# Fused attention, dense layer and eight experts: float32r and bf16 words become pairs of float16 parts

## The chip, the core and the metric

The kernel runs on one core of a Trainium2 chip (trn2). A core has TensorE (PE, with its weight loads shown apart as PEld), VectorE (DVE), ScalarE (ACT), GpSimd (POOL) and SyncE (SP, which here mostly starts transfers), and 16 DMA engines. The metric is the time of one execution on the device in microseconds.

## The reference

Three parts follow each other; the output of one is the input of the next, always with 1152 tokens of 512 numbers.

```python
# attention: batch 2, 8 heads, 576 positions, head size 64
scores = scale * np.matmul(q, k.transpose(0, 1, 3, 2))
cum = np.cumsum(np.maximum(s, 0.0), axis=-1)
bias = -(cum[:, :, :, None] - cum[:, :, None, :])
scores = np.where(causal, -1000000000.0, scores + np.minimum(bias, 0.0))
x = softmax(scores) @ v
# dense layer, 512 -> 2048 -> 512; w_in and w_out arrive as 64-bit floats
h = x @ w_in
x2 = (h * (1.0 / (1.0 + np.exp(-1.702 * h)))) @ w_out
# experts: the best of 8 for each token, at most 288 tokens each
expert_idx = np.argmax(x2 @ w_gate, axis=1)
y = np.maximum(disp @ w1, 0.0) @ w2          # 512 -> 1024 -> 512
out[i] = gate_w[i] * y[expert_idx[i], pos[i]]
```

The results have to be close to float32, so that the kernel splits numbers into parts, and a product of two numbers is made of three products of parts: high by high, high by low, and low by high.

## The kernel before

**How the order is made.** The program text calls `pl.op(engine, cost, function, r=, w=, rank=)`. Class `Plan` collects these operations, takes the dependences from the keys in `r` and `w`, and a list scheduler with modelled costs writes each engine's instructions in the order that it finds: among the operations that are ready, the one with the lowest rank goes first. Ranks come from the stage (`n + 0.5`, `base + 15` and the like) plus a table `SHIFT` of hand-tuned offsets. On the chip each engine then goes through its own list in that order, and waits for others by semaphores.

**Attention** (0 to about 130 us) works on 8 pairs of heads. A `unit` takes one pair and one tile of queries t (64 rows for t=0, 128 for t=1 to 4): PE makes the scores in float32 (`score_mm`, L863, and the causal mask with L864), DVE takes the maximum (L885), ACT the exponential (`pexp`, L894), and the result is split into two float16 parts in the tile `ph` (L846 and L848, with POOL or DVE at L908 and L913). SP sends `ph` through a DMA transpose into `PT` (L921), in blocks of 128x128, and `av_unit` multiplies by the values (L941, float16). Two heads give 128 columns; PE transposes them (L965), and three copies go to `xT` (high and low, float32r) and `xTb` (bf16, L846).

**Dense layer** (92 to about 330 us). The 1152 tokens are three chunks of 384, the 2048 inner numbers 16 blocks of 128. `mm1` for a chunk c and a block fc runs 8 float32r matmuls of 384 columns (L577, high weights by high and low x) and 4 bf16 matmuls (L581, low weights by high x), then ACT tanh, DVE, ACT high part, DVE low part (L585 to L591), and one more ACT copy in bf16 (`gtB`, L594). `mm2` runs for each tile of 128 tokens two float32r matmuls of 512 columns (L610) and one of bf16 (L611). There are 48 of the former and 144 of the latter. `w_conv` makes each block of weights out of 64-bit words with bit operations on ACT and DVE and a subtraction on POOL or DVE (L536 to L553). `logits` transposes a tile of x2, copies it to SBUF and multiplies by `w_gate` in float32 (L1208). `route` counts and sends rows to the memory `xs_d`.

**Experts** (335 to 470 us) come sorted by their number of tokens, with compiled widths WR = (224, 200, 184, 168, 152, 144, 136, 128). `w_unit` loads 512 KB pieces of weights in a ring of buffers, ACT makes the high part (L1455) and DVE the low part (L1456). `xs_in` fetches an expert's rows (x2R<-xs_d), transposes and splits them (L1535 on). `e_mm1` has 8 units an expert, `e_mm2` 4. Their float32r matmuls hold high and low side by side, 2w columns (L1569, L1606), the bf16 matmuls the narrower width that the run has counted, by a register on PE (`widths`, `held`, L1573, L1608). Afterwards the halves of PSUM are added: ACT copies one half (L1583), DVE adds (L1585), ACT relu (L1587), DVE low part (L1589), ACT bf16 copy (L1592). `e_mm2` is left by ACT (L1613) and DVE (L1615). The last expert is computed by rows (`e_row`, L1634), ending in `e_out_row` (L1669) and an indirect DMA (L1642). Behind all of it stands a branch for experts with more tokens than the compiled width (L1738), which isn't taken.

## Time and profile before

| | us |
|---|---|
| median of three executions | 487.0 |
| the three | 487.0, 2492.14, 484.84 |
| profiled execution | 485.11 |
| its span | 483.4 |
| PE busy | 458.7 |
| DVE, ACT, POOL busy | 362.7, 332.4, 122.9 |

The span lasts from the first to the last instruction recorded on the core; the profiled execution's own time has the start and end around it too. PE means matmuls; a weight load can run beside the matmul before it, so the two don't add up. "PEclk" is the clock granted to TensorE as a share of 2.4 GHz. "DMA" is the share of the time in which the 16 DMA engines were busy. The chain of waits is made backwards from the last instruction: each piece is the work that the next one waited for.

### The profile page before, as it was taken

The page shows a single profiled execution, that of the slowest core. Times are in us where ns is not written, and L with a number is a line of the kernel's source. Part 1 is how long each engine was busy: PE and PEld are TensorE (multiplying, and loading weights), DVE is VectorE, ACT ScalarE, POOL GpSimd, SP SyncE. Part 2 cuts the span into 40 slices and gives each one's busy share as a digit, 9 for nine tenths or more (in the row PEclk, how much of TensorE's full clock was granted, in tenths as well). Part 3 has the DMA queues.
Part 4 walks back from the last instruction along what each step waited for, and adds up shares of the span by engine and source line. Part 5 has one row for each costly group of instructions (what it writes and reads, how often), then busy time and mean ns, then how long its engine had stood idle before and what let it go on. Part 6 is the DMA issues. An engine that isn't in the chain of part 4 may idle for free.

```text
span 483.4 us, 9843 instructions
## 1 busy us (share of the span) xinstructions
PE 458.7 (95%) x3458; PEld 349.3 (72%) x3460; DVE 362.7 (75%) x826; ACT 332.4 (69%) x785; POOL 122.9 (25%) x136
## 2 busy tenths in 40 slices
PE   8898898999999999999999999999989999999993
PEld 7465566667777667768766867668868888979982
DVE  6889678988989999963224365956977979989991
ACT  3778979887667676753235346843878979989981
POOL 5437667467221231210000040001100201111141
PEclk9979999999999999999999999999999999999997
DMA  7998999699964554990000068840694858888811
GB/s 162 275 224 186 223 211 185 165 174 188 214 226 135 171 159 154 360 265 0 2 0 1 4 238 310 291 154 10 200 346 135 284 181 261 278 288 246 279 71 41
DMA packets 99049, 88.22 MB, mean 183 GB/s; under 512 B 66679, under 2 KB 77943, under 8 KB 98982
## 3 DMA queue, kind: packets, MB, share of 16 engines
q1 hardware_dynamic: 97108, 82.04, 62.1%
q0 software_dynamic: 1888, 5.52, 3.0%
q8 instruction: 28, 0.46, 0.4%
q14 instruction: 25, 0.20, 0.1%
HBM read 60.60 MB, written 14.19 MB: 155 GB/s over the span
## 4 chain that ended last, share of the span: by engine, by line
PE 73%; ACT 8%; DMA 7%; issue 4%; DVE 4%; POOL 2%; POOLq 0%; SPq 0%; ACTq 0%; DVEq 0%
PE SC L610 11%; PE MI L577 8%; PE MX L577 6%; PE AV L1606 6%; PE SC L611 5%; PE SC L863 5%; DMA PT<-ph 4%; PE MI L581 4%; PE MI L1569 3%; PE AV L610 3%; PE MX L581 3%; PE MX L1569 3%; PE AV L941 3%; PE AV L1608 2%; ACT pexp L894 2%
## 5 line engine op out<-in xcount | busy, mean ns | idle before, releaser
L610 PE MATMUL SC<-woH,gtH 128*128 128x512 f32 x212 | 76.6, 479 | 0.0
L863 PE MATMUL SC<-QK 128*128 128x512 f32 (+4 forms) x192 | 64.7, 444 | 3.4 <-ACT pexp L894 3.4
L908 POOL TENSOR_TENSOR ph<-pexp,ph 128x512 f16<-128x512 f32 (+4 forms) x32 | 44.8, 1400 | 30.0 <-DVE ph L848 18.4
L591 DVE SCALAR_TENSOR_TENSOR gtH<-th,gtH 128x384 fp32r<-128x384 f32 x46 | 26.1, 569 | 32.8 <-ACT gtH L589 32.1
L894 ACT ACTIVATE pexp<-SC,smA 64x64 f32<-64x64 f32 (+4 forms) x80 | 38.2, 520 | 13.8 <-DVE smA L885 12.1
L577 PE MATMUL MI<-xT,wiH 128*128 128x384 f32 x216 | 47.1, 357 | 0.0
L594 ACT ACTIVATE gtB<-th 128x384 bf16<-128x384 f32 x46 | 23.8, 519 | 32.0 <-PE SC L611 26.1
L610 PEld LDWEIGHTS SC<-woH,gtH 128*128 128x128 f32 x212 | 40.0, 194 | 3.3
L1456 DVE TENSOR_TENSOR wiL<-wraw,wiH 128x1024 bf16<-128x1024 f32 x32 | 38.8, 1218 | 3.5 <-ACT wiH L1455 3.5
L611 PE MATMUL SC<-woL,gtB 128*128 128x512 bf16 x106 | 41.4, 390 | 0.0
L1456 DVE TENSOR_TENSOR woL<-wraw,woH 128x1024 bf16<-128x1024 f32 x32 | 38.9, 1217 | 3.1 <-ACT woH L1455 3.1
L863 PEld LDWEIGHTS SC<-QK 128*128 128x128 f32 (+1 forms) x192 | 28.9, 192 | 15.9 <-issue 8.2
L611 PEld LDWEIGHTS <-gtB 128*128 128x128 bf16 x138 | 13.3, 96 | 37.5 <-issue 37.5
L1271 POOL DMA_INDIRECT xs_d<-x2R,small x9 | 9.0, 997 | 121.2 <-ACT x2Tt L1204 69.2
L577 PEld LDWEIGHTS MI<-xT,wiH 128*128 128x128 f32 x216 | 38.0, 189 | 1.3 <-DVE th L587 0.3
L553 POOL TENSOR_TENSOR wiL<-wvi,wiH 128x512 bf16<-128x512 f32 x16 | 22.1, 1383 | 64.7 <-ACT wiH L549 64.7
L1642 POOL DMA_INDIRECT out_dram<-x2R,small x8 | 9.1, 1133 | 114.4 <-ACT x2R L1669 65.6
L577 PE MATMUL MX<-xT,wiH 128*128 128x384 f32 x168 | 36.7, 359 | 0.0
L1455 ACT ACTIVATE wiH<-wraw 128x1024 fp32r<-128x1024 f32 x32 | 33.6, 1055 | 2.0 <-DMA wraw<-in_moe_w_dram 2.0
L1455 ACT ACTIVATE woH<-wraw 128x1024 fp32r<-128x1024 f32 x32 | 34.0, 1063 | 0.5 <-DMA wraw<-in_moe_w_dram 0.5
L577 PEld LDWEIGHTS MX<-xT,wiH 128*128 128x128 f32 x168 | 30.0, 189 | 0.8
L941 PE MATMUL AV<-V,PT 128*128 128x65 f16 (+1 forms) x640 | 25.6, 195 | 5.1 <-DMA PT<-ph 4.4
(280 smaller groups left out, 1149.1 us busy)
## 6 DMA issues: line engine op xcount, KB each, us to landing
wraw<-in_moe_w_dram SPq DMA_DIRECT2D x64, 512.0 KB
wraw<-in_moe_w_in_dram SPq DMA_DIRECT2D x16, 512.0 KB
wraw<-in_moe_w_out_dram SPq DMA_DIRECT2D x16, 512.0 KB
xs_d<-x2R SPq DMA_DIRECT2D x16, 257.0 KB
kraw<-in_k_dram SPq DMA_DIRECT2D x8, 288.0 KB
qraw<-in_q_dram SPq DMA_DIRECT2D x8, 288.0 KB
out_dram<-x2R SPq DMA_DIRECT2D x9, 256.0 KB
x2R<-xs_d SPq DMA_DIRECT2D x8, 257.0 KB
```

The source lines that it names most:

```text
L577: nc.tensor.matmul(ps, lhsT=whi[:, kc], rhs=xT[:, a, kc, cs], start=(kc == 0 and a == 0), stop=False)
L581: nc.tensor.matmul(ps, lhsT=wlo[:, kc], rhs=xTb[:, kc, cs], start=False, stop=(kc == KC - 1))
L610: nc.tensor.matmul(o, lhsT=gh[:, a, ts], rhs=whi, start=(fc == 0 and a == 0), stop=False)
L611: nc.tensor.matmul(o, lhsT=gb[:, ts], rhs=wlo, start=False, stop=(fc == NFC - 1))
L863: nc.tensor.matmul(o[:rows, j0:j1], lhsT=t_[:, 2 * r, i0:i0 + rows], rhs=t_[:, 2 * r + 1, j0:j1], start=True, stop=False)
L894: pl.op("act", t_act(wdt, False, 1), lambda o=o, r=r, nm=nm: nc.scalar.activation(out=pe[:rows, r, :wdt], in_=o[:rows, :wdt], func=AF.Exp, ...
L908: pl.op(eng, (t_pool if eng == "pool" else t_dve)(n * T_), lambda rs_=rs_, e_=e_: e_.tensor_tensor(out=hl[:, rs_, 0:T_], in0=pe[:rows, rs_ ...
L941: nc.tensor.matmul(av[:, slot, r, 0:D + 1 - h_], lhsT=PT[t][:, r * (1 + 2 * t) + pb, :], rhs=rhs, start=(i == 0), stop=(i == len(m) - 1))
L1455: pl.op("act", t_act(1024), lambda: nc.scalar.activation(out=dhi, in_=raw, func=AF.Copy), r=[rk], w=kh, rank=rank, after=after)
L1456: pl.op("dve", t_dve(1024), lambda: nc.vector.tensor_tensor(out=dlo, in0=raw, in1=dhi.bitcast(F32), op=ALU.subtract), r=[rk, ks[0], ks[2]] ...
L1569: nc.tensor.matmul(ps[:, 0:2 * w_], lhsT=uH[s_][kc][:, fs], rhs=xs[:, kc], start=(kc == 0), stop=False)
L1606: nc.tensor.matmul(ps[:, 0:2 * w_], lhsT=uH[s_][KC + fc // 2][:, ds_[fc]], rhs=h[:, fc], start=(fc == 0), stop=False)
```

## The change

- The dense layer's and the experts' weights and inputs (`wiH`, `wiL`, `woH`, `woL`, `gtH`, `xT`) become float16, scaled by powers of two. Each product is three float16 matmuls into one PSUM region. The bf16 copies `gtB`, `xTb` and those of the experts are gone.
- In the experts the high and the low half are no longer side by side: 2w columns of float32r and the counted width in bf16 become three matmuls of w columns. ACT relu and DVE subtraction are what is left of the five operations; the first expert's units rotate over four PSUM banks instead of two. `widths` is gone.
- Range checks: many DVE and a few ACT operations also sum up what they write (`accum_out`) in `acc`; `good` squares, compares and sends one flag. A second branch behind the first holds `general`, a whole float32 path of some 580 instructions, which isn't taken for these inputs.
- `logits3` splits x2 in three bf16 parts and multiplies by three bf16 parts of `w_gate` (12 matmuls of 24 columns) for chunks 0 and 1. Chunk 2 keeps the float32 `logits`.
- In attention the tile t=0 of both heads of a pair becomes one tile of 128 rows (`first`); `ph01` has 7 blocks instead of 8. Tile t=4 has scores of 288 and 288 columns instead of 512 and 64.
- The last expert's output is scaled half on ACT and half on DVE.
- `SHIFT` is a new table of rank offsets, some 200 lines before and after; the diff below begins with one line of each.

```diff
-    "a.bias_keep.sp.cumd": 32.2, "a.bias_keep.sp.cumd@": -40, "a.bias_rows.sp.QKb@": -25.5,
+    "a.bias_keep.sp.cumd@": 4.4, "a.bias_rows.sp.QKb": 29.8, "a.consts.a.pool.identF": -24, "a.consts.b.pool.": 29.9,
...
     def weights(pool, ji, jo):
         for j in ji:
-            wiH[j] = pool.tile([P, 2, KC, GF], F32R, name=f"wiH{j}")
-            wiL[j] = pool.tile([P, 2, KC, GF], BF16, name=f"wiL{j}")
+            wiH[j] = pool.tile([P, 2, KC, GF], F16, name=f"wiH{j}")
+            wiL[j] = pool.tile([P, 2, KC, GF], F16, name=f"wiL{j}")
...
     def mm1(pl, n, c, fc, bank, bk, deps=()):
...
-                nc.tensor.matmul(ps, lhsT=wlo[:, kc], rhs=xTb[:, kc, cs], start=False, stop=(kc == KC - 1))
+                nc.tensor.matmul(ps, lhsT=wlo[:, kc], rhs=xT[:, 0, kc, cs], start=False, stop=(kc == KC - 1))
...
-        pl.op("act", t_act(CN), lambda: nc.scalar.activation(out=gb, in_=th, func=AF.Copy, scale=0.5),
-              r=[("th", n % 2)], w=[("gtb", gi)] + xw)
...
     def mm2(pl, n, c, fc, tt, bk):
...
-            nc.tensor.matmul(o, lhsT=gb[:, ts], rhs=wlo, start=False, stop=(fc == NFC - 1))
+            nc.tensor.matmul(o, lhsT=gh[:, 0, ts], rhs=wlo, start=False, stop=(fc == NFC - 1))
...
-            pl.op("dve", t_dve(1024), lambda: nc.vector.tensor_tensor(out=dlo, in0=raw, in1=dhi.bitcast(F32), op=ALU.subtract),
+            pl.op("dve", t_dve(1024) + 65, lambda: nc.vector.scalar_tensor_tensor(
+                out=dlo, in0=raw, scalar=SE, in1=dhi, op0=ALU.mult, op1=ALU.subtract, accum_out=total),
...
         def e_mm1(e, fc, i=None):
-            s_, w_, hk = e % 2, WR[e], fc % 2
+            s_, w_, hk = e % 2, WR[e], fc % (2 if e else 4)
...
             def mmh():
                 for kc in range(KC):
-                    nc.tensor.matmul(ps[:, 0:2 * w_], lhsT=uH[s_][kc][:, fs], rhs=xs[:, kc], start=(kc == 0), stop=False)
+                    nc.tensor.matmul(ps, lhsT=uH[s_][kc][:, fs], rhs=xs[:, kc, 0], start=(kc == 0), stop=False)
+                    nc.tensor.matmul(ps, lhsT=uH[s_][kc][:, fs], rhs=xs[:, kc, 1], start=False, stop=False)
...
-            pl.op("act", t_act(w_, False), lambda: nc.scalar.activation(out=tl, in_=ps[:, w_:2 * w_], func=AF.Copy),
-            pl.op("dve", t_dve(w_), lambda: nc.vector.tensor_tensor(out=sm, in0=ps[:, 0:w_], in1=tl, op=ALU.add),
-            pl.op("act", t_act(w_), lambda: nc.scalar.activation(out=hh, in_=sm, func=AF.Relu),
-            pl.op("dve", t_dve(w_), lambda: nc.vector.scalar_tensor_tensor(out=hl, in0=sm, scalar=0.0,
-            pl.op("act", t_act(w_), lambda: nc.scalar.activation(out=hb_, in_=sm, func=AF.Relu),
+            pl.op("act", t_act(w_, False), lambda: nc.scalar.activation(out=hh, in_=ps, func=AF.Relu), r=[bk], w=[("hT", s_, fc)])
+            pl.op("dve", t_dve(w_) + 65, lambda: nc.vector.scalar_tensor_tensor(
+                out=hl, in0=ps, scalar=0.0, in1=hh, op0=ALU.max, op1=ALU.subtract, accum_out=acc[:, A_H, ac:ac + 1]),
...
+        def logits3(c, tt):
...
+            pl.op("act", t_act(512, False), lambda: nc.scalar.activation(out=xs_[0], in_=b_, func=AF.Copy), r=[bk], w=[("x2q", 0)])
+            pl.op("dve", t_dve(512), lambda: V.tensor_tensor(out=b_, in0=b_, in1=xs_[0], op=ALU.subtract), r=[("x2q", 0)], w=[bk])
+            pl.op("act", t_act(512, False), lambda: nc.scalar.activation(out=xs_[1], in_=b_, func=AF.Copy), r=[bk], w=[("x2q", 1)])
+            pl.op("dve", t_dve(512), lambda: V.tensor_tensor(out=xs_[2], in0=b_, in1=xs_[1], op=ALU.subtract), r=[bk, ("x2q", 1)], w=[("x2q", 2)])
...
-    ph01 = ap_.tile([P, 8 * P], F16, name="ph01")
+    ph01 = ap_.tile([P, 7 * P], F16, name="ph01")
...
-        copy(XTB, m, xTb[:, p, t0_:t0_ + m], xT[:, 0, p, t0_:t0_ + m].bitcast(F32), r=[("xT", x_, t)], w=[("xTb", x_, t)])
...
+    n_bad = nc.values_load(ovi[0:1, 9:10], min_val=0, max_val=1)
+    with tc.If(n_bad > 0):
+        general()
```

What this moves is seen at three places. The first is PE in the middle of the dense layer, before. MI, MX and SC are PSUM banks; a float32r matmul carries its weight load in its own row, a bf16 one has a row for it.

```order
L577 MATMUL MI<-xT,wiH_1937 128x384 x8
L581 LDWEIGHTS wiL_1938
L581 MATMUL MI<-xTb,wiL_1938 128x384
...
L610 MATMUL SC_105<-woH_1945,gtH 128x512 x2
L611 LDWEIGHTS gtB
L611 MATMUL SC_105<-woL_1946,gtB 128x512
```

The same place after.

```order
L606 LDWEIGHTS gtH
L606 MATMUL SC_106<-woH_1903,gtH 128x512
...
L607 LDWEIGHTS gtH
L607 MATMUL SC_106<-woL_1904,gtH 128x512
L573 LDWEIGHTS wiH_1895
L573 MATMUL MX<-xT,wiH_1895 128x384
...
L577 LDWEIGHTS wiL_1896
L577 MATMUL MX<-xT,wiL_1896 128x384
```

Units of `mm1` and triples of `mm2` still alternate; each matmul has a weight load of its own in front of it now. The second place is PE in the second expert (width 200), before.

```order
L1569 MATMUL MI<-xT,woH_82 128x400
L1569 MATMUL MI<-xT,woH_1692 128x400
L1569 MATMUL MI<-xT,woH_1945 128x400
L1569 MATMUL MI<-xT,woH_1947 128x400
L1573 LDWEIGHTS woL_83
L1573 MATMUL MI<-xTb,woL_83 128x200
```

And after.

```order
L1628 LDWEIGHTS woH_83
L1628 MATMUL MX<-xT,woH_83 128x200
L1629 LDWEIGHTS woH_83
L1629 MATMUL MX<-xT,woH_83 128x200
...
L1633 LDWEIGHTS woL_84
L1633 MATMUL MX<-xT,woL_84 128x200
```

Four matmuls of 400 columns became eight of 200, and the same weights are loaded twice. The third place is ACT in the first expert, before; wvi_94 and wvi_95 are the buffers for one half of PSUM and for the sum.

```order
L1455 ACTIVATE woH_1951<-wraw_1687 128x1024
L1583 ACTIVATE wvi_94<-MI 128x96
L1587 ACTIVATE xT<-wvi_95 128x96
L1592 ACTIVATE xTb<-wvi_95 128x96
L1583 ACTIVATE wvi_94<-MX 128x96
L1587 ACTIVATE xT<-wvi_95 128x96
L1592 ACTIVATE xTb<-wvi_95 128x96
L1455 ACTIVATE woH_1953<-wraw_1688 128x1024
```

And after.

```order
L1544 ACTIVATE woH_1909<-wraw_1666 128x1024
L1643 ACTIVATE xT<-AV_107 128x96
L1643 ACTIVATE xT<-AV_108 128x96
L1643 ACTIVATE xT<-MI 128x128
L1544 ACTIVATE woH_1911<-wraw_1667 128x1024
```

Each unit has one ACT row instead of three, it reads PSUM directly, and between two conversions of weights stand three units instead of two.

## Rows read from the trace of the kernel before

**Rows 1.** Busy time per engine, from the profile's first part.
```profile
PE 458.7 (95%) x3458; PEld 349.3 (72%) x3460; DVE 362.7 (75%) x826; ACT 332.4 (69%) x785; POOL 122.9 (25%) x136
```

**Rows 2.** Windows: length, busy PE, PEld, DVE, ACT, POOL; PEclk, DMA share, GB/s.
```profile
60.00:80.00 20.00, 17.50 (x230) 12.37 (x229) 16.56 (x30) 17.20 (x40) 13.72 (x14) 1.00 0.98 193
...
120.00:140.00 20.00, 20.00 (x180) 14.51 (x177) 18.89 (x40) 12.13 (x25) 5.49 (x8) 1.00 0.90 226
...
240.00:260.00 20.00, 20.00 (x105) 14.30 (x104) 5.00 (x9) 5.72 (x12) 0.00 (x0) 1.00 0.00 1
...
340.00:360.00 20.00, 16.58 (x148) 14.48 (x148) 17.14 (x65) 16.30 (x55) 1.12 (x2) 1.00 0.83 266
...
440.00:460.00 20.00, 20.00 (x207) 18.69 (x206) 19.15 (x42) 19.16 (x53) 1.90 (x2) 1.00 0.86 264
```

**Rows 3.** Chain of waits in attention: start us, us, what.
```profile
57.88 9.11 DMA PT<-ph x2
...
96.16 1.50 PE AV L941 x50
```

**Rows 4.** Instructions of L941 and L755: count, duration min/median/max in ns.
```profile
L941 PEld LDWEIGHTS <-PT x640: 95/97/151, 25.9 to 133.4; 128*128 128x128 f16 x160
...
L755 DVE DVE_READ_ACCUMULATOR gtB<-vraw x2: 75/79/83, 8.1 to 9.0; 128x1 f32 x2
```

**Rows 5.** Chain of waits in the second expert's start.
```profile
362.92 1.82 PE AV L1606 x8
364.74 0.78 PE AV L1608 x8
365.52 0.74 PE MI L1569 x4
366.26 0.28 PE MI L1573 x4
```

**Rows 6.** Chain of waits in the middle of the dense layer.
```profile
231.62 1.41 PE MI L577 x8
233.04 0.67 PE MI L581 x4
233.70 0.46 PE AV L610 x2
234.16 0.23 PE AV L611
```

**Rows 7.** Chain of waits at the first logits, and at 8-column bf16 matmuls.
```profile
273.34 0.79 PE AV L1208 x8
...
284.44 0.05 PE AV L1245 x2
```

**Rows 8.** Chain of waits late in the experts (widths 136 and 144).
```profile
444.39 0.55 PE MX L1569 x4
444.94 0.23 PE MX L1573 x4
...
445.94 1.11 PE AV L1606 x8
447.05 0.47 PE AV L1608 x8
```

**Rows 9.** Chain of waits in the first expert.
```profile
343.73 0.24 ACT wvi L1583
...
346.61 0.95 ACT woH L1455
...
351.79 5.07 DMA x2R<-xs_d
```

**Rows 10.** Chain of waits at the end.
```profile
472.65 3.79 issue
...
476.50 0.51 POOLq L1738
```

More of the change, by code (lines that the diff above doesn't have):

```diff
@@ L231 @@
+    "b.w_conv.low.dve.wraw@x": -4.6, "b.w_conv.main.act.wo": 7.4, "b.w_conv.main.act.wo@x": 9.9,
+    "b.w_conv.rest.dve.wo": -5.3, "b.w_conv.sign.dve.wvi": 17.2, "b.w_conv.top.act.wvi": -2.4,
+    "b.w_load.load.sp.wraw": 10.5, "b.w_load.load.sp.wraw@x": -3.3, "b0.consts.pool.acc": 8.8,
[128 rows of a table added]
+    "c.first_load.load.sp.x2r": -21.3, "c.first_rows.dve.sel": -22.8, "c.first_rows.mm.pe.BK": 0.9,
[55 rows of a table added]
 }
@@ L445, in fused_kernel @@
     xc_d = dram.tile([P, XR], F32, name="xc_d")
+    xh_d = dram.tile([H, NT, D], F32, name="xh_d")
     cum_d = dram.tile([B * NPR, 2, 4, S], F32, name="cum_d")
@@ L517, in w_conv @@
         key = ("wi" if kind == "in" else "wo", g)
-        xh = xl = []
-        if g // 2 == NPW - 1:
-            i_ = NGT + (kind == "out")
-            xh, xl = [("gt", i_), ("gtl", i_)], [("gtb", NGT), ("gtb", NGT + 1)] if kind == "out" else []
+        xh = [(x, NGT + (kind == "out")) for x in ("gt", "gtl")] if g // 2 == NPW - 1 else []
+        sums = {} if g not in (10, 12) else dict(accum_out=acc[:, A_WI if kind == "in" else A_WO, g:g + 1])
         vi = wvi[n % NVI]
@@ L867, in unit @@
     def unit(x_, t):
+        if not t:
+            return first(x_)
         i0, rows = TI[t]
@@ L977, in dense @@
         pl.rank += dr
-        mm1(pl, n, *m1s[n], MI, ("BK", 0), [(x, b * NPR + p, t) for x in ("xT", "xTl", "xTb") for p in range(NPR)
+        mm1(pl, n, *m1s[n], MI, ("BK", 0), [(x, b * NPR + p, t) for x in ("xT", "xTl") for p in range(NPR)
                                        for b, t in (((0, 2), (0, 4)), ((0, 4), (1, 2)))[c]])
@@ L1085, in fused_kernel @@
         srt2 = bp.tile([P, 2 * E], F32, name="srt2")
-        cntI = bp.tile([P, E], I32, name="cntI")
-        WMIN = 64
-        wreg = [nc.tensor.shape_register(n) for n in range(E)]
-        ytl = [x2r[4][:, i * W:(i + 1) * W] for i in range(2)]
+        stat = bp.tile([P, 2, 64], F32, name="stat")
+        lgj = bp.tile([P, CT * E], F32, name="lgj")
+        gd = bp.tile([P, 1], BF16, name="gd")
         zrow = x2r[3]
@@ L1368, in fused_kernel @@
         eid = {}
+        gates()
         while wstate["load"] < wstate["conv"] + NRW:
@@ L1571, in mml @@
             def mml():
                 for kc in range(KC):
-                    nc.tensor.matmul(held(e, ps[:, 0:w_]), lhsT=uL[s_][kc][:, fs], rhs=held(e, xb_[:, kc]), start=False, stop=(kc == KC - 1))
-            wk = [((nm, 2 * kc + g), a) for kc in range(KC) for g in range(2) for a in (0, 1, 3)] + xk + (["wreg"] if e else [])
+                    nc.tensor.matmul(ps, lhsT=uL[s_][kc][:, fs], rhs=xs[:, kc, 0], start=False, stop=(kc == KC - 1))
+            wk = [((nm, 2 * kc + g), a) for kc in range(KC) for g in range(2) for a in (0, 1, 3)] + xk
```

541 lines of the change are left out of this document (355 added, 186 removed), and 381 rows, old and new, of the table SHIFT.

## The prediction

> **What bounds the kernel now.** I read the share of each engine first, then the table by 20 us windows, then the chain of waits stage by stage. TensorE is busy for 95% of the span [rows 1]. The windows divide the span into four stages [rows 2]. In the first 120 us, attention, PE has gaps (17.5 of 20 us) while the DMA share is near 1. From 120 to 340 us, the dense layer, PE is busy 20.00 of 20 us in every window, and at 240 DVE and ACT need only 5 to 6: there PE alone sets the time, and a shorter matmul stream is a shorter kernel. From 340 to 360, the first expert, PE has 3.4 us of gaps, while ACT is at 16.3 and DVE at 17.1. From 360 to 470 PE is full again, but DVE and ACT stand at 19.1 each in 440 to 460 and the DMA share is 0.86: whatever is taken from PE there soon meets the other three.
>
> **The change, part by part.** All sums are made against the profiled execution, 485.1 us with a span of 483.4, so 1.7 us lie around it. It is 0.3 above the lowest and 1.9 below the median of the three times shown.
>
> *Pitch of a float16 matmul.* No matmul of before has the new form (float16, each with its own weight load, 96 to 512 columns), so I take bf16 and narrow float16 rows, which also load before each matmul. 50 attention matmuls of 64 or 65 columns took 1.50 us, 30 ns each [rows 3]: 27 ns of columns at 2.4 GHz and 3 more, though a weight load is recorded with 97 ns [rows 4]. Eight bf16 matmuls of 224 columns took 0.78 us, 97 ns each [rows 5], again columns and 4 ns. Four of 384 took 0.67, 167 each, one of 512 took 0.23 [rows 6]; each of those runs ends in a change back to the float32r kind, so they are an upper bound. I take columns/2.4 and 3 ns: 163 at 384, 216 at 512.
>
> *Dense layer.* A first multiplication is 8 float32r and 4 bf16 matmuls now, 1.41+0.67 = 2.08 us; after it is 12 of 163 ns, 1.96 (−0.12; bounds −0.07 with 167 and −0.16 with bare columns). There are 48: −5.8 us. A triple of the second is 0.46+0.23 = 0.69; after, 3 of 216, 0.65 (−0.04; bounds 0 and −0.05). There are 144: −6.2. Together **−12** (−3 to −15), nearly all of it in windows where PE has no gap. The bf16 copy that ACT loses (L594) and the few DVE sums for the range flag count as nothing there: PE's own work hides both, with ACT at 12.1 and 5.7 and DVE at 18.9 and 5.0 of 20 in the windows from 120 and 240. That cover is thin on DVE from 120: if a conversion of weights came late there, PE would wait for `wiL`, and part of the 12 would go.
>
> *Logits.* A tile of float32 logits takes 0.79 us of PE [rows 7]. Six of the nine tiles become 12 bf16 matmuls of 24 columns, 12 x 30 ns = 0.36 (the 64-column row; lower bound 8-column matmuls at 25, 0.30): −0.45 each, **−2.7** (−1 to −3.2, since ACT and DVE splits of 512 columns come between, beside a PE that has other work).
>
> *Experts, PE.* Per unit of e_mm1 at width 200 now 0.74+0.28 = 1.02 us, after 12 x (83+3) = 1.04: nothing. At width 136, 0.55+0.23 = 0.78, after 12 x (57+3) = 0.72 [rows 5, 8]. The low part is narrowed at run time now and is full width after, which is why the wide ones gain nothing; I take −0.05 as the mean over 56 units, −2.8. e_mm2 at width 224 is 1.82+0.78 = 2.60 and becomes 24 x 96 = 2.31; at 144 it is 1.11+0.47 = 1.58 and becomes 24 x 63 = 1.51. The wide piece holds a gap, so I take −0.1 over 28, −2.8. **−5** in round numbers (−2 to −7).
>
> *Experts, ACT and DVE.* In 340 to 351 the chain runs over ACT: each unit of the first expert asks for L1583 (0.24), L1587 and L1592, between weight conversions L1455 of 0.95 [rows 9]. After, one ACT relu and one DVE operation remain per unit. 16 units x 2 operations x about 0.25 us are 8 us less ACT work in that stretch. PE could give back its 3.4 us of gaps and some of the stretched units; then the wait for the second expert's rows follows (5.07 us, [rows 9]) with the DMA share at 0.83 [rows 2], and a faster start moves it earlier only as far as the weight transfers allow. I take **−4** (0 to −6). In the rest DVE loses one of two operations per unit (some 0.3 us x 8 per expert) and the add of e_mm2, and gains an accumulator read of 0.08 us on 16 instructions [rows 4]: clearly less than 19.1 of 20, so it doesn't become the bound; ACT still less.
>
> *Attention.* The merged first tile sends 49 instead of 50 blocks through the DMA transposes per pair (2%), and the 16 `xTb` copies leave ACT, which is at 17.2 of 20. The chain goes through waits for PT, the longest piece 9.1 us [rows 3], which 2% of the blocks hardly changes. The new table of ranks moves all else by a little, and I can't price it: **−3**, with +3 and −8 as bounds (8 is half of the 20.0 − 17.5 us by which PE falls short in each of six windows; 3 is a third of the longest wait for PT, should the order make one more).
>
> *Tail.* The flag is made beside the last output; the second load of a register and its branch stand behind the first. The first branch stands on the chain with 0.51 us and is preceded by 3.8 of issue [rows 10]. I take **+1** (0.5 to 4: the lower bound is the branch alone, the upper one a second such stretch). In the Trainium skill, "Runtime: NRT & Kernel Launch", section Instruction fetch mechanics, a taken branch out of the prefetched pages forces a fetch before execution goes on, and the jump over the new float32 path is such a one; it would lie inside that range.
>
> Sum: −12 −2.7 −5 −4 −3 +1 = −25.7; span 457.7, time **459**.
>
> **Rivals.** (A) Transfers bind. If attention keeps its length and the start of the experts stays with the x2R transfer and weight loads, terms −3 and −4 fall away: 466 us. For it: DMA share near 1 in attention and 0.83 to 1 in 340 to 360. (B) Attention follows its lighter ACT: with −8 there and bounds of −15 in the dense layer, 459 −5 −3 = 451. (C) Slower: the weight load in front of each narrow matmul is not hidden, and no matmul starts sooner than one load of 97 ns after the last. The widths below 224 then cost 97 ns each: 192 matmuls an expert at 200, 184, 168, 152, 144, 136 fall short by 11, 17, 24, 31, 34 and 37 ns (30 us in all), the 96 of width 128 by 41 (4), the first expert's 96 of width 96 and 96 of 128 by 54 and 41 (9): +43, so 502. A floor of 77, halfway between a load and the 56 that 128 columns take, would by the same count cost 16: 475. It decides from a floor of about 85 ns, where the cost reaches the 26 us gained. Against it stand 30 and 97 ns at 64 and 224 columns [rows 3, 5]. The Trainium skill, "TensorE: Matmul & The Clock Gate", section Back-to-back issue gap, speaks for a weaker form of it: a stream of load and matmul pairs goes at about 81 ns each at 128 columns, where the columns alone would give 56. With a floor of 81 instead of 97 the same widths would cost about 20 us, an estimate from that page, and the time would be near 479. The 64-column row with 30 ns disagrees, so I give it little. (D) Nothing much: ranks and checks lose in attention (+3) and the tail (+4) while dense gives only its lower bound (−3), logits −1, experts −2: 486.
>
> **How the numbers follow.** Forecast 453 to 463: 0.42. A, 463 to 472: 0.25. B, below 453: 0.18. Between A and D, or C with the halfway floor, 472 to 477: 0.04. C whole, over 495: 0.04; D, 477 to 495: 0.07. Predicted is the likeliest, 459. From 447 to 472 holds some 0.8, a little of B cut off below. About 2% (10 us) is what a measurement of this kernel can tell from no change. Faster 0.88, same 0.07, slower 0.05.
>
> **What would show it.** The first multiplication of the dense layer at 1.95 to 2.0 us and its triple at 0.65 in the chain around the middle; PE without a gap until the dense layer ends, 15 us earlier than now counted from its start; a 128-column matmul start to start at 56 and not at 97 ns; PE over 19 of 20 us in the first window of the experts; DVE and ACT below 17 of 20 late in the experts; PT waits as long as now; behind the last output about 1 us more. I am wrong if 512-column float16 matmuls stay at 230 ns, if narrow ones have a floor, if the new order leaves gaps in PE between 120 and 340, or if the end of the experts waits on transfers.

## The result and the profile after

| | before | after |
|---|---|---|
| median of the runs shown, us | 487.93 | 470.57 |
| lowest to highest | 484.84 to 2492.14 | 469.34 to 472.33 |
| ratio, 95% interval | | 0.9667 (0.9601 to 0.9734) |
| profiled execution | 485.11 | 471.46 |
| its span | 483.4 | 469.7 |

The change is worth 17 us in the medians and 13.7 us in the two profiled spans. The execution of 2492.14 us counts as a slow run and stays out of the ratio. The time lies inside the forecast range (447 to 472), but near its upper end: 12 us of the 25.7 forecast are missing. The first part of the page of the kernel after answers to [rows 1]:

```profile
PE 430.4 (92%) x3980; PEld 309.3 (66%) x3980; DVE 346.2 (74%) x906; ACT 275.6 (59%) x569; POOL 121.8 (26%) x147
```

PE is busy for 28.3 us less, ACT for 56.8 less, DVE for 16.5 less. The span fell by half of what PE lost; the rest became idle time of PE. The windows that answer to [rows 2] (same columns) show where:

```profile
60.00:80.00 20.00, 16.00 (x200) 12.20 (x199) 16.29 (x38) 15.21 (x38) 12.65 (x14) 0.99 1.07 189
120.00:140.00 20.00, 18.99 (x193) 11.71 (x192) 17.68 (x40) 9.66 (x19) 6.79 (x12) 1.00 1.01 233
240.00:260.00 20.00, 20.00 (x150) 12.17 (x149) 11.60 (x34) 10.74 (x24) 0.00 (x0) 1.00 0.01 1
...
400.00:420.00 20.00, 19.51 (x280) 18.84 (x278) 16.76 (x47) 15.72 (x30) 3.05 (x2) 1.00 0.81 280
...
440.00:460.00 20.00, 18.44 (x242) 15.14 (x239) 13.37 (x44) 9.63 (x21) 4.77 (x5) 1.00 0.16 54
```

The dense layer at 240 still has PE full, though DVE and ACT have twice the work there; attention at 60 has more gaps than before (16.00 instead of 17.50), and late in the experts DVE and ACT are below 17 of 20, as forecast (16.76 and 15.72 at 400; the window at 440 already holds the end of the last expert). The first expert has moved ahead of 340, so it is compared in its own stretch, from its first matmul to its first `e_mm2`, before and then after:

```profile
335.00:354.40 19.40, 16.66 (x166) 15.36 (x167) 18.19 (x90) 15.27 (x59) 3.75 (x4) 1.00 0.63 203
```

```profile
321.00:336.30 15.30, 15.17 (x250) 14.87 (x248) 14.07 (x102) 7.55 (x24) 4.10 (x12) 1.00 0.42 136
```

PE's gaps there went from 2.7 us to 0.1, and ACT's work from 15.3 us to 7.6.

To place the difference I cut both traces at the same points of the program (start of the matmul named, in us from the start of the span; one profile of each):

| start of | before | after | stage, after − before | forecast |
|---|---|---|---|---|
| the 7th first multiplication (attention done but for its end) | 141.8 | 141.3 | −0.5 | −3 |
| the last second multiplication (dense layer, logits) | 330.3 | 318.6 | −11.2 | −14.7 |
| the first expert's first matmul | 335.0 | 321.0 | −2.3 | none |
| its first `e_mm2` | 354.4 | 336.3 | −4.1 | −4 |
| the last matmul of the last expert's output | 475.3 | 457.8 | +0.6 | −5 |
| end of the span | 483.4 | 469.7 | +3.8 | +1 |

The sums of the prediction are right for the streams that PE works through. In the chain of waits in the dense layer, answering to [rows 6], a first multiplication is 1.30+0.65 and a triple 0.43+0.21:

```profile
234.07 1.30 PE MX L573 x8
235.37 0.65 PE MX L577 x4
...
236.67 0.43 PE SC L606 x2
237.10 0.21 PE SC L607
```

That is 1.95 and 0.65 us, as forecast. The logits in bf16 triples, answering to [rows 7], take 0.29 us instead of 0.79, and narrow matmuls with a weight load each, answering to [rows 8], follow each other at their columns and a little:

```profile
273.35 0.29 PE SC L1267 x12
...
437.47 0.50 PE AV L1662 x8
...
450.95 0.22 PE MI L1633 x4
```

Eight of 144 columns take 0.50 us, 62 ns each; four of 128 columns take 0.22, 56 each. The weight loads in front of them are recorded with a mean of 98 ns, and are hidden: no matmul waits for one.

### The profile page after: what moved, and what is told of

Same layout as the page of the kernel before. It is cut to its first block, busy times and chain, and to the rows that moved or that the text cites. A ratio compares the mean times of both kernels' runs of the same rounds, so it can differ in the third digit from the quotient of the medians.

```text
span 469.7 us, 10693 instructions
## 1 busy us (share of the span) xinstructions
PE 430.4 (92%) x3980; PEld 309.3 (66%) x3980; DVE 346.2 (74%) x906; ACT 275.6 (59%) x569; POOL 121.8 (26%) x147
## 4 chain that ended last, share of the span: by engine, by line
PE 54%; DMA 14%; DVE 12%; issue 11%; POOL 3%; ACT 2%; SPq 2%; POOLq 0%; DVEq 0%; ACTq 0%
PE SC L606 8%; PE MI L573 6%; PE SC L861 5%; PE MX L573 5%; DMA PT<-ph 4%; PE SC L607 4%; PE MI L577 3%; DMA wraw<-in_moe_w_dram 3%; PE AV L960 3%; DMA wraw<-in_moe_w_in_dram 3%; PE MX L577 2%; PE AV L606 2%; DMA out_dram<-x2R,small 2%; POOL out_dram L1692 2%; DVE wvi L540 1%
## 5 line engine op out<-in xcount | busy, mean ns | idle before, releaser
L606 PE MATMUL SC<-woH,gtH 128*128 128x512 f16 x212 | 63.0, 379 | 0.0
L573 PEld LDWEIGHTS <-wiH 128*128 128x128 f16 x384 | 37.0, 98 | 29.7 <-issue 3.5
L861 PE MATMUL SC<-QK 128*128 128x288 f32 (+3 forms) x160 | 55.1, 473 | 0.3 <-ACT pexp L917 0.3
L930 POOL TENSOR_TENSOR ph<-pexp,ph 128x512 f16<-128x512 f32 (+4 forms) x32 | 44.0, 1378 | 16.5 <-issue 9.7
L1546 DVE SCALAR_TENSOR_TENSOR wiL<-wraw,wiH 128x1024 f16<-128x1024 f32 x32 | 38.8, 1221 | 11.4 <-ACT wiH L1544 11.4
L573 PE MATMUL MI<-xT,wiH 128*128 128x384 f16 x216 | 40.8, 326 | 1.7 <-DVE th L583 1.7
L1544 ACT ACTIVATE wiH<-wraw 128x1024 f16<-128x1024 f32 x32 | 33.3, 1054 | 15.2 <-DMA wraw<-in_moe_w_dram 15.0
L1546 DVE SCALAR_TENSOR_TENSOR woL<-wraw,woH 128x1024 f16<-128x1024 f32 x32 | 38.6, 1217 | 4.3 <-ACT woH L1544 4.3
L917 ACT ACTIVATE pexp<-SC,smA 128x192 f32<-128x192 f32 (+3 forms) x64 | 34.3, 579 | 12.4 <-DVE smA L905 6.7
L607 PE MATMUL SC<-woL,gtH 128*128 128x512 f16 x106 | 40.2, 379 | 0.0
L1544 ACT ACTIVATE woH<-wraw 128x1024 f16<-128x1024 f32 x32 | 33.3, 1054 | 2.8 <-DMA wraw<-in_moe_w_dram 2.8
L960 PEld LDWEIGHTS <-PT 128*128 128x128 f16 x640 | 23.8, 101 | 13.1 <-DMA PT<-ph 11.2
L838 ACT ACTIVATE QK<-MI 64x288 f32<-64x288 f32 x57 | 24.3, 426 | 10.5 <-DVE QK L841 5.3
```

Source lines behind the costliest of these rows:

```text
L573: nc.tensor.matmul(ps, lhsT=whi[:, kc], rhs=xT[:, a, kc, cs], start=(kc == 0 and a == 0), stop=False)
L606: nc.tensor.matmul(o, lhsT=gh[:, a, ts], rhs=whi, start=(fc == 0 and a == 0), stop=False)
L607: nc.tensor.matmul(o, lhsT=gh[:, 0, ts], rhs=wlo, start=False, stop=(fc == NFC - 1))
L838: pl.op("act", t_act(3 * TQ, False) + 130, lambda o=o, in_=in_, sc=sc: nc.scalar.activation(out=o, in_=in_, func=AF.Copy, scale=sc), r=[bk ...
L861: nc.tensor.matmul(o, lhsT=t_[:, 2 * r, i0:i0 + rows], rhs=t_[:, 2 * r + 1, j0:j0 + n], start=True, stop=(j0 + n <= i0))
L917: pl.op("act", t_act(wdt, False, 1), lambda o=o, e=e, r=r, nm=nm: nc.scalar.activation(out=e, in_=o, func=AF.Exp, bias=nm[:rows, r:r + 1]) ...
```

## The experiments

Each is compared with the kernel before, run beside it. Stages are those of the table above, read from one profile of each.

### Eight small tiles for the experts' row data instead of four

In the kernel after, DVE waits in the middle of the experts for something that never held it before. Its waits from 320 to 458 us (engine, line, releaser: us in total, times, longest):

```profile
DVE small L1607 <- DMA out_dram<-x2R,small: 9.2, 4, 3.1
```

L1607 copies an expert's token numbers and gate weights into one of four small tiles, `meta[e % 4]`. The indirect DMA that scatters the expert four before reads that tile, so the copy waits until the scatter has landed. The chain of waits, then DVE's timeline, then PE's:

```profile
421.60 7.62 DMA out_dram<-x2R,small
```

```profile
429.24 0.17 DVE L1607 COPY small<-x2R 128x2 f32<-128x2 f32 x1 [3.10 <-DMA out_dram<-x2R,small]
429.32 1.23 DVE L1546 SCALAR_TENSOR_TENSOR wiL<-wraw,wiH 128x1024 f16<-128x1024 f32 x1
...
430.47 0.29 DVE L1644 SCALAR_TENSOR_TENSOR xT<-MI,xT 128x136 f16<-128x136 f32 x1
```

```profile
430.83 0.22 PE L1628 MATMUL MI<-gtH,wiH 128*128 128x136 f16 x1 [2.46 <-DVE xT L1644]
```

Behind the waiting copy, DVE's written order holds a conversion of weights and the low part that PE needs (L1644). PE stands for 2.46 us.

```diff
-        small = bp.tile([P, 2 * 200 + 16], F32, name="small")
-        meta = [small[:, 400 + 4 * i:404 + 4 * i]... for i in range(4)]
+        small = bp.tile([P, 2 * 200 + 32], F32, name="small")
+        meta = [small[:, 400 + 4 * i:404 + 4 * i]... for i in range(8)]
...
-                ... nc.vector.tensor_copy(out=meta[e % 4][:n, j, :], ...
+                ... nc.vector.tensor_copy(out=meta[e][:n, j, :], ...
```

> The changed kernel with one edit: the small buffer that holds an expert's gates and token numbers (meta) exists eight times instead of four; every engine's order is the same, row by row. Theory (the experts lost their gain to one false wait): in the changed kernel DVE stood 9.2 us in 4 waits at the two-column copy L1607 until a scatter (out_dram) that reads the old meta had landed, the longest 3.1 us at 426 us, with a PE gap of 2.5 us and a stretch at half clock (0.66 in 430 to 435) behind it. Without it these waits vanish, the gap at 428 us too, and the time falls by 3 to 5 us, to 465.5 to 467.5. Rival (the weight transfers bind the late experts, DMA share 0.8 to 0.94): DVE then waits for weights instead, the gap stays under another name, and the time is within 1 us of the changed kernel's 470.6.

Measured: 467.38 us (464.49 to 470.6), ratio 0.9603 (0.9553 to 0.9654). The wait is gone; DVE's L1607 waits only for the expert's rows to arrive:

```profile
DVE small L1607 <- DMA x2R<-xs_d: 2.6, 3, 1.6
```

The same two windows, of the kernel after first, then of this one:

```profile
425.00:430.00 5.00, 3.37 (x54) 3.23 (x52) 1.91 (x6) 3.41 (x8) 0.02 (x1) 1.00 0.92 363
430.00:435.00 5.00, 4.17 (x40) 4.10 (x40) 5.00 (x16) 3.34 (x6) 0.00 (x0) 0.66 0.55 133
```

```profile
425.00:430.00 5.00, 5.00 (x79) 4.91 (x77) 4.27 (x15) 3.98 (x9) 1.62 (x1) 1.00 1.00 353
430.00:435.00 5.00, 5.00 (x83) 4.93 (x81) 4.42 (x13) 5.00 (x11) 0.00 (x0) 1.00 0.94 295
```

With four tiles PE idles, and right behind the idle time the granted clock is 0.66 (part of the stretch at 1.2 instead of 2.4 GHz). With eight, PE is full and at full clock. The stretch from the first `e_mm2` to the last matmul is 117.4 us instead of 121.5. The mechanism is shown. Its price is less sure: the intervals of the two ratios (0.9553 to 0.9654 here, 0.9601 to 0.9734 for after) overlap. Of the seven kernels below that keep four tiles and the new table, one (K loaded earlier) has the same picture as after: a gap of 2.33 us, half clock behind it, and 121.9 us for this stretch. The other six have gaps of 1.2 to 1.5 us at this place, no half clock behind them, and 117.9 to 119.3 us, each in a single profile. So the wait costs at most some 2 us of the stretch by itself, and some 4 where the clock falls behind it.

### Without the second branch and the float32 path behind it

```diff
-    n_bad = nc.values_load(ovi[0:1, 9:10], min_val=0, max_val=1)
-    with tc.If(n_bad > 0):
-        general()
```

> The changed kernel without its second register load and branch and without the float32 path behind it (so nothing is done when the flag says that the range is left); sums and flag are still made. Theory (the second branch costs what the tail lost, 3.3 us from the start of the last scatter to the end, 9.96 instead of 6.7 us): the last scatter lands after 3.1 us as in the kernel before and not after 5.4, the 4.6 us branch of PE is gone, and the time falls by 2.8 to 3.5 us. Rival (the scatter lands late for another reason, and the branch lies beside it): less than 1.2 us.

Measured: 467.36 us (466.21 to 469.88), ratio 0.964 (0.9593 to 0.9688). From the start of the last matmul to the end it takes 10.1 us; after has 11.9, before 8.1. In the kernel after, the compare-and-branch rows of PE's sequencer, of the second branch and of the first (count: duration min/median/max in ns):

```profile
L1983 PEldq COMPARE_BRANCH  x1: 4617/4617/4617, 461.4 to 461.4; - x1
```

```profile
L1796 PEldq COMPARE_BRANCH  x1: 373/373/373, 460.4 to 460.4; - x1
```

PE's jump over the float32 path takes 4.6 us, its first one 0.37. The code that is fetched can be seen in the DMA queue of instructions from the last row on, of after (8 us) and of before (6 us; queue, kind: packets, MB, share):

```profile
q14 instruction: 9, 0.07, 3.7%
```

```profile
q14 instruction: 1, 0.01, 0.3%
```

The Trainium skill, "Runtime: NRT & Kernel Launch", section Instruction fetch mechanics, says that a taken branch out of the prefetched pages makes a fetch necessary before execution goes on; these rows agree. But the 4.6 us are not on the way to the end in this profile. The end follows POOL, which waits for the last scatter to land, loads the second flag, branches, and closes the kernel. INC_SWDGE_SEM is its first row behind the landing, DRAIN begins the closing (duration ns min/median/max, first and last start in us):

```profile
L1796 POOLq INC_SWDGE_SEM  x1: 696/696/696, 465.1 to 465.1; - x1
L1982 POOLq TENSOR_LOAD <-maskB x1: 316/316/316, 465.8 to 465.8; - x1
L1983 POOLq COMPARE_BRANCH  x1: 45/45/45, 466.2 to 466.2; - x1
L2013 POOLq DRAIN  x3: 44/107/2115, 466.7 to 469.4; - x3
```

PE's jump lies beside this, from 461.4 to 466.0. The tail's +3.8 us are three pieces. The last scatter starts 1.9 us behind the last matmul's start instead of 1.4; it lands 5.3 us after its start instead of 3.1; and the second load and branch put 0.9 us on POOL behind it. Without the second branch the third piece is gone and the landing takes 4.4 us: 1.8 us of the 3.8. The landing did not go back to 3.1, as the expectation had it. The first piece is the flag: two of its reductions (L1392, L1393) stand on DVE ahead of the half of the last output that DVE makes (L1709).

```profile
458.63 0.28 DVE stat L1393
...
458.94 0.48 DVE x2R L1709
```

Why the scatter lands late, no run settles. It takes 4.1 to 6.2 us in the eight profiles that show it with half of the last output made on DVE, with the second branch or without. It takes 3.1 in before and 2.7 in the last kernel below, where ACT makes that output alone; no run changes this alone.

### Also without the sums of the range check

The `accum_out=` of the conversions, activations and evacuations is left out too, 144 reads on DVE and 10 on ACT, and with it the sums that the range check needs.

> The same as the run without the second branch, and no sums are made beside the conversions, activations and evacuations (every accumulation left out, so the flag is made of zeros and not used); the order is the same. It differs from that run by 64 + 72 accumulator reads of 0.08 us on DVE in the experts and some on ACT. Theory (DVE and ACT are no bound any more, DVE at 13 to 17 of 20 us): within 1 us of the run without the branch. Rival (sums lengthen the chains that PE waits for in the experts' start, 16 units one after the other, and the conversions): 2 to 4 us faster than it.

Measured: 468.56 us (466.22 to 473.43), ratio 0.9681 (0.9611 to 0.9751), beside 0.964 (0.9593 to 0.9688) for the same kernel with sums. The sums cost nothing that can be measured, as the prediction had it.

### K and q of the seventh pair loaded earlier

The two loads move some eight places up in SP's order, to about 67 us; in after, PE waits for K (2.8 us in three waits).

```diff
+        sel = [n for n in order if ops[n][0] == "sp" and "qk_load" in ops[n][2].__qualname__]
+        vl = [n for n in order if ops[n][0] == "sp" and "v_load" in ops[n][2].__qualname__]
...
+            for n in sel[12:14]:
+                order.remove(n)
+                at = order.index(vl[-2])
...
+                order.insert(at, n)
```

> The changed kernel with one edit: the k and q loads of the seventh pair of heads, which SP issued at 78.4 us behind weight loads and transposes, stand 8 rows earlier on SP, at about 67 us, where their buffers are free; all else keeps its order. Theory (the order by the new table held PE back there: a wait of 1.9 us for kraw at 81.8, and the granted clock 0.51 from 80 to 90 us behind it, which is 5 us of half speed): the wait and most of that stretch at half clock vanish, and the time falls by 3 to 6 us. Rival (attention is bound by the DMA transposes, DMA share over 1 there): the wait moves to PT or to the delayed value loads, and the time is within 1.5 us.

Measured: 469.43 us (466.19 to 473.91), ratio 0.9637 (0.957 to 0.9703). The attention stage ended at 138.3 instead of 141.3 us in the profile, but the two kernels above, which leave attention as it is, show 139.4 and 140.1. PE still waits 2.6 us for K, in two waits. The half clock that after has from 80 to 90 us (0.51) is not there (1.00), without a gain clear of noise. Inconclusive: at most some 1 to 3 us.

### The first two conversions of expert weights behind the next dense steps

The only large gap of PE in the dense layer of after lies at 291.5 us. ACT's row ahead of it, DVE's timeline, and PE's row:

```profile
288.49 1.06 ACT L1544 ACTIVATE wiH<-wraw 128x1024 f16<-128x1024 f32 x1 [6.20 <-DMA wraw<-in_moe_w_dram]
```

```profile
291.25 1.22 DVE L1546 SCALAR_TENSOR_TENSOR wiL<-wraw,wiH 128x1024 f16<-128x1024 f32 x1
...
292.40 0.55 DVE L583 SCALAR_TENSOR_TENSOR th<-th,MI 128x384 f32<-128x384 f32 x1
```

```profile
293.00 1.46 PE L573 MATMUL MI<-xT,wiH 128*128 128x384 f16 x8 [1.51 <-DVE th L583]
```

ACT had waited 6.2 us for a piece of expert weights, with dense steps queued behind that conversion; then conversions and dense steps follow each other in both queues while PE waits for a free PSUM bank. The edit moves the first two conversions behind the next three dense steps on ACT and the next two on DVE.

```diff
+            for eng, skip in (("act", 3), ("dve", 2)):
+                w = named(eng, "w_unit")[0:2]
+                at = order.index(w[0])
+                m = [n for n in order[at:] if ... "mm1" in ops[n][2].__qualname__.split(".")][skip - 1]
...
+                p_ = order.index(m) + 1
+                order[p_:p_] = w
...
```

> The changed kernel with one edit: on ACT the first two weight conversions of the experts (L1544, which wait for their transfer from 282 to 288.5 us) stand behind the next three activations of the dense layer instead of ahead of and between them, on DVE the two subtractions L1546 behind the next two dense steps. Theory (PE's gap of 1.4 to 2.1 us at 290, found in every run of the changed kernel and not before, comes from dense work queued behind conversions that wait for a late transfer): the gap falls below 0.3 us, the last matmul of the dense layer comes 1.3 to 2 us sooner, and the time falls by 1 to 2 us. Rival (the gap is the latency of tanh, DVE and the copies themselves): it stays above 1 us.

Measured: 469.82 us (468.36 to 473.69), ratio 0.9671 (0.9607 to 0.9736): no difference from after. The gap moved with the conversions, from 293.00 to 295.45:

```profile
290.93 1.23 DVE L1570 SCALAR_TENSOR_TENSOR wiL<-wraw,wiH 128x1024 f16<-128x1024 f32 x1 [0.45 <-ACT wiH L1568]
...
292.08 1.22 DVE L1570 SCALAR_TENSOR_TENSOR wiL<-wraw,wiH 128x1024 f16<-128x1024 f32 x1
...
293.23 0.55 DVE L613 SCALAR_TENSOR_TENSOR gtH<-th,gtH 128x384 f16<-128x384 f32 x1
```

```profile
295.45 1.46 PE L597 MATMUL MX<-xT,wiH 128*128 128x384 f16 x8 [1.30 <-DVE th L607]
```

Two conversions in a row now stand ahead of another dense step (L613). A burst of conversions has to fit between dense steps; moving it whole doesn't help.

### The table of ranks of before under the new instructions

The edit puts the `SHIFT` of before (its diff is the whole table) into the kernel after.

> The changed kernel with the rank offsets (SHIFT) of the kernel before, whose names fit most of the operations; nothing else. Theory (the offsets fit one kernel's costs: they are worth several us, and what attention lost by the new ones is small beside it): slower than the changed kernel by 5 to 20 us, with gaps in PE from 120 to 340. Rival (the new table put attention into a worse order, which ate the forecast 3 us): attention (until the seventh first multiplication, 141 us) is 2 us or more shorter than with the new table, and the whole is within 5 us.

Measured: 503.29 us (501.48 to 503.42), ratio 1.0321 (1.0261 to 1.0381): 33 us slower than after, and slower than before. Attention takes 8 us more (149.4), the dense layer with its logits 16 more (193.5 instead of 177.3), the rest of the difference lies in the experts and the tail. Among PE's gaps are three of this kind, 2.8 to 3.0 us, in the logits:

```profile
287.88 0.47 PE L1276 MATMUL AV<-wgq,x2Tt 128*128 128x24 bf16 x12 [2.82 <-DVE x2Tt L1271]
```

PE's written order reaches the multiplication before the two splits on ACT and DVE are through. So the cheaper instructions alone don't make a faster kernel here: the old ranks fit other instructions. The 33 us are not the price of tuning alone, though: 335 of the old table's 780 names aren't in the new one, and operations that only after has, such as these logits, get no offset from the old table.

### The float32 logits of before in all three chunks

```diff
-                            logits3(c_, tt)
+                            logits(c_, tt)
```

> The changed kernel with the float32 logits of before for chunks 0 and 1 as well (the bf16 parts of w_gate are still made, and not used); the list scheduler makes a new order for it. Theory (the stretch is bound by PE): from the 24th first multiplication to the last matmul of the dense layer it takes 2.5 to 3.2 us longer, 6 x (0.79 - 0.29), and so does the whole, but for what the new order does in the experts. Rival (the split's two activations and two subtractions of 512 columns a tile take back what PE saves): within 1 us in that stretch.

Measured: 479.54 us (474.59 to 488.56), ratio 0.9844 (0.9769 to 0.992), some 9 us above after; its four runs spread over 14 us. From the 25th first multiplication to the end of the dense layer it takes 108.4 us instead of 102.2, 6.2 more. Of that 3.0 are the matmuls themselves (six times 0.79 − 0.29). Another 3.4 us are a stretch in which PE is full and the granted clock is 0.50:

```profile
252.50:259.30 6.80, 6.80 (x41) 5.09 (x40) 3.65 (x27) 2.24 (x5) 0.90 (x1) 0.50 0.30 116
```

PE has no gap ahead of it; the first float32 logits start at 249.5. Before, with the same logits, shows 1.00 from 120 to 460 us, and the scheduler wrote another order for this kernel, so whether the stretch comes from the logits or from the order stays open. PE's gaps in the stage (1.8 us) are no larger than in after (2.2). The forecast −2.7 for the logits agrees with 3.0.

### One transpose in four sent twice

Two runs. Here a DMA transpose of the merged tiles t=0 and t=1 (7 blocks) is sent a second time into a tile that nobody reads.

```diff
+    PTz = ap_.tile([P, 7, P], F16, name="PTz")
...
-            pl.op("sp", 0, lambda o=o, i=i: nc.sync.dma_start_transpose(out=o, in_=i),
+            def send(o=o, i=i):
+                nc.sync.dma_start_transpose(out=o, in_=i)
+                if o is PT01:
+                    nc.sync.dma_start_transpose(out=PTz, in_=i)
+            pl.op("sp", 0, send,
```

> The changed kernel, with the DMA transpose of the merged tiles t=0 and t=1 (7 blocks) sent twice for each of the 8 pairs, the second time into a tile that nobody reads: 56 blocks more beside 392, 14%. No other instruction is added and the written order of every engine stays. Theory: the transfers set the length of attention, so that 2% fewer blocks could give back at most about 2 us and the lighter ACT nothing. By the rows of the changed kernel the transposes land a median of 5.8 us after their issue; if a block takes some 0.1 us of the queue, 56 more cost 5 to 8 us, and the seventh first multiplication of the dense layer comes at 146 to 149 us instead of 141.3; total 475 to 479. Rival: the chain over ACT, DVE and POOL from scores to split sets the length, and transfers have slack: the seventh first multiplication stays at 139 to 142.5, total 468 to 473.

Measured: 495.48 us (491.7 to 497.93), ratio 1.014 (1.0055 to 1.0224), and attention until 163.6 instead of 141.3. These 22 us are not the transposes alone: `Plan` builds the keys of `SHIFT` from function names, the new name `send` took the transposes out of the table, and SP's order changed. The second run keeps the name, and with it every engine's order:

```diff
+            twice = [nc.sync.dma_start_transpose] if t == 1 else []
-            pl.op("sp", 0, lambda o=o, i=i: nc.sync.dma_start_transpose(out=o, in_=i),
+            pl.op("sp", 0, lambda o=o, i=i, twice=twice: (nc.sync.dma_start_transpose(out=o, in_=i),
+                                                          [f(out=PTz, in_=i) for f in twice]),
```

> As the run before, 7 blocks sent twice for each of the 8 pairs into a tile that nobody reads, but now every engine keeps the written order of the changed kernel exactly (in the run before a new function name changed the keys by which the table of ranks finds its operations, and with them the order, so that its 22 us in attention are doubled transposes and another order together). Theory, transfers set the length of attention: 56 more blocks cost 5 to 8 us, the seventh first multiplication of the dense layer at 146 to 149 instead of 141.3, total 475 to 479. Rival, transfers have slack: the seventh first multiplication at 139 to 142.5, total 468 to 473; the 22 us of the run before were then nearly all order.

Measured: 477.24 us (476.29 to 479.62), ratio 0.9829 (0.9785 to 0.9873). Attention ends at 149.8 instead of 141.3, 8.5 us for 56 blocks or 0.15 a block, and the end comes 6.7 us later in the medians. So the transposes have no slack: what is added to them makes attention longer. It need not be the 16 DMA engines that are full. Each of the eight extra issues takes a median of 1.38 us of SP's queue, and the loads behind them come later: the K loads of the last two pairs are issued at 85.2 and 93.6 us instead of 78.4 and 86.1, and PE's waits for K grow from 2.8 to 6.5 us, those for `PT` only from 8.3 to 9.3. Nor are transfers alone on the way: in after SP's transposes wait 41 us in all for the split parts from POOL. The run doesn't tell these apart. The first of the two runs then says by the way that 14 us more (163.6 − 149.8) came from the lost ranks of one operation.

### Everything together

Eight small tiles, the earlier K, the moved conversions, one outer branch around both paths (its flag is the sum of the two flags), and the last output whole on ACT instead of half on ACT and half on DVE:

```diff
+            dv(75, lambda: V.tensor_tensor(out=ovi[0:1, 10:11], in0=ovi[0:1, 9:10], in1=ovi[0:1, 8:9], op=ALU.add), ["ov"], "flag")
...
+    n_any = nc.values_load(ovi[0:1, 10:11], min_val=0, max_val=NT // P + E + 1)
+    with tc.If(n_any > 0):
...
-            pl.op("act", t_act(h_, False, 1), lambda: nc.scalar.activation(out=y[:, 0:h_], in_=BK[XB[0][0]][:, 0:h_], ...
-            pl.op("dve", t_dve(h_) + 67, lambda: nc.vector.tensor_scalar(out=y[:, h_:], in0=BK[XB[0][0]][:, h_:], ...
+            pl.op("act", t_act(DM, False, 1), lambda: nc.scalar.activation(out=y, in_=BK[XB[0][0]], ...
```

> The changed kernel with five edits, the order else the same: eight meta buffers; the k and q loads of the seventh pair earlier on SP; the first two weight conversions of the experts on ACT and DVE behind the next tanh and its DVE step instead of ahead of them; both branches inside one outer branch, whose register is the sum of the two flags; and the last output wholly on ACT, so that DVE has the flag alone. Theory (each wait that was found is real and they add up): 3 to 4 us in the experts, 1 to 3 in attention, 1.5 to 2 in the dense layer, 1 to 2 in the tail: 461 to 464 us, below both kernels and below each single edit. Rival (waits take each other's place; executions differ by 3 us anyway): 465 to 468.

Measured in seven runs: 465.3 us (464.54 to 467.77), ratio 0.9551 (0.9509 to 0.9593). That is faster than after by some 5 us, with intervals that don't overlap, and beats both kernels, but it is the rival's 465 to 468 and not the sum of the single gains. In its profile attention ends at 142.1 and the dense stage takes 177.2 us, as in after; the experts take 118.4 instead of 121.5. The chain at its end runs from the last matmul over ACT alone to the scatter, 10.5 us to the end instead of 11.9:

```profile
455.95 0.70 ACT x2R L1739
...
456.92 1.00 POOL out_dram L1725
```

The scatter lands in 2.7 us, at 459.6. But PE's jump still takes 4.2 us, and POOL stands behind its own branch until 461.8: here the one outer branch does hold the end, by 2 to 3 us.

```profile
L1825 POOLq COMPARE_BRANCH  x1: 53/53/53, 458.3 to 458.3; - x1
L1825 POOLq EVENT_SEMAPHORE  x6: 17/30/43, 461.8 to 462.3; - x6
```

## Why the prediction came out as it did

The time fell inside the range, but not where the forecast had it: 470.6 lies in the stretch that the prediction gave to rival A (463 to 472, 0.25) and not in its own (453 to 463, 0.42). Of A one half came true, attention, and the other, the first expert, did not. What was missing came from terms that the prediction had mis-sized, and 2.3 us that it had not foreseen made up for part of it; that the total still fell inside is in part luck.

**Dense layer and logits, −12 and −2.7: right, 3.5 us short.** The stage gave 11.2 instead of 14.7. The unit prices were exact for the dense layer (1.95 and 0.65), and the logits came out cheaper than forecast (0.29 instead of 0.36 us), so that the stream gave about −14. PE had no gap in this stage before and has some 2.9 us of gaps after; the largest, 1.51 us, is the one at 293. Gaps between 120 and 340 were one of the prediction's own signs of being wrong. It had named the cause ("if a conversion came late"), but at the wrong conversion: it was not the dense weights at 120 us but the experts' weights at 290, where [rows 2] has no window: its row at 240 showed DVE and ACT with air, and the prediction took that for the whole end of the stage. Where the gap can be closed, no run showed. Yet full engines alone don't make the gap. Before had DVE at 18.61 and ACT at 17.26 of 20 us from 300 to 320, and PE without a gap; what after has is dense steps queued behind conversions.

**Pitch of narrow matmuls, and rival C: settled.** At 128 and 144 columns the matmuls come every 56 and 62 ns. No weight load of 98 ns shows through. The Trainium skill, "TensorE: Matmul & The Clock Gate", section Back-to-back issue gap, gives about 81 ns for pairs of load and matmul at 128 columns; the trace doesn't agree, it has 56. The rule drawn from 64-column attention rows [rows 3] held.

**First expert, −4: right.** The stretch up to its first `e_mm2` fell from 19.4 to 15.3 us, 4.1: 2.6 of it are PE's gaps, the rest its own work, and ACT's work fell by 7.7 us beside the 8 that were forecast. The step from the end of the dense layer to the first matmul gave 2.3 more (4.7 to 2.4), which I hadn't foreseen: in after PE begins the expert ahead of the last tile's logits, in before behind them.

**Experts on PE, −5: mis-sized; the stream was right, the waits were not.** The stage came out at +0.6 in this profile. PE's gaps rose from 1.7 to 4.7 us, and the clock of 0.66 from 430 to 435 costs 5 × 0.34 = 1.7 more; without these 4.7 the stream gave about −4, close to the forecast. The largest of the gaps, 2.46 us, is the wait for the scatter. The half clock behind it came in two of the eight kernels with four tiles and the new table; the other six have 117.9 to 119.3 us, 1.5 to 2.9 below before, so that the + sign is this profile's. In before, the same tiles existed, and nothing waited for them. I had costed DVE and ACT only by their busy time, and asked whether they become the bound. They don't (16.76 and 15.72 of 20 us in the window at 400); but a DVE that runs earlier reaches a tile before its reader, a DMA, is done with it.

**Attention, −3: mis-sized, −0.5.** In four other kernels with the same attention this point comes at 139.4 to 141.4 us, so the gain lies between 0.4 and 2.5. ACT became lighter, and PE's waits for its exponentials nearly went away. The waits of PE in the first 141 us, of before and then of after:

```profile
PE AV L941 <- DMA PT<-ph: 4.4, 5, 1.4
PE SC L863 <- ACT pexp L894: 3.4, 8, 0.7
...
PE MI L832 <- DMA QK<-cum_d: 1.0, 1, 1.0
...
PE MI L832 <- DMA kraw<-in_k_dram: 0.3, 1, 0.3
```

```profile
PE AV L960 <- DMA PT<-ph: 8.3, 9, 1.9
PE MI L832 <- DMA kraw<-in_k_dram: 2.8, 3, 1.9
PE SC L875 <- DMA QK<-QK: 2.8, 1, 2.8
...
PE SC L861 <- ACT pexp L917: 0.3, 1, 0.3
```

The waits for exponentials fell by 3.1 us, those for transfers rose from 5.7 to about 14. The doubled transposes show that they have no slack; by 0.15 us a block the 8 blocks that the change saves are worth 1.2 us, of the size that was seen. The value in rival A (nothing) was the better one, and the DMA share near 1 in [rows 2], which the prediction quotes, pointed that way. The new order stands in this stage too, and no run tells its part from that of the lighter ACT. The bound of −8 was also worked out too wide: the six windows of before fall short by 12.4 us together, not 15, since the last two have 19.28 and 18.84 of 20; half of that is 6.

**Tail, +1: wrong in size, +3.8,** near the upper bound given (0.5 to 4), and that it fell inside is luck, because [rows 10] was misread. Its 0.51 us of L1738 are POOL's load of the flag and not a branch, and its 3.8 us of issue are POOL's wait for ACT's last output (L1654), while PE was still at work:

```profile
L1738 POOLq TENSOR_LOAD <-maskB x1: 507/507/507, 476.5 to 476.5; - x1
```

```profile
POOL out_dram L1642 <- ACT x2R L1654: 4.0, 1, 4.0
```

Neither was the price of a second branch. What the runs show in their place is 0.9 us of POOL for the second load and branch, 0.5 for the flag, which stands not beside the last output but ahead of half of it, and 2.3 for the scatter's landing, whose cause stays open.

**The order.** The prediction allowed the new table a loss of 3 us in attention and priced it nowhere else. With the old table the same instructions take 33 us more, and the kernel would have been slower than before; no row of before could show how well the new table fits.

## What to carry to other kernels

Price a shorter instruction stream by its rows, and then look for what the faster engines will arrive at too early: buffers still being read by a DMA, and bursts of work in the same queue. In a stage whose DMA share was near 1, a lighter engine gave back at most 2.5 us here. Before a row of the chain is taken as a price, look up what the row is: a load, a wait or a branch. Where a planner writes the order, ranks belong to the instructions they were tuned for, and even a renamed function can undo them.

## What the hardware showed unexpectedly

- A float16 matmul of 128 or 144 columns with a 98 ns weight load in front of each runs at 56 or 62 ns.
- A branch taken over a long piece of code that isn't run holds PE's sequencer for 4.6 us (4.2 to 5.0 in the other profiles with it); over a short one 0.37. It costs the kernel this time only where the end waits for it, as with the one outer branch (458.3 to 461.8 on POOL), and not where a scatter lands later.
- An indirect scatter of an expert's rows takes up to 7.62 us before its index tile is free, and the last one 2.7 to 6.2 us to land.
- In the two profiles where PE stood 2.3 to 2.5 us for the late scatter, the granted clock went to half for 3.4 us behind it; in the six where it stood 1.2 to 1.5 us there, the clock stayed at 1.00.
